# Fused attention, gated feed-forward and DFT mixing: 64-bit weights become 32-bit in three VectorE steps instead of four, and the scheduler is handed smaller pieces of the exponentials and of the w_out products

## The chip, the cores and the metric

The kernel runs on one core of one Trainium2 chip. Its engines, with the names that the profile gives them, are TensorE (PE, with its weight loads as PEld), VectorE (DVE), ScalarE (ACT), GpSimd (POOL) and SyncE (SP), which issues the DMAs of this kernel. Each engine works through its own instructions in the order in which they were written; engines wait for one another through semaphores. The metric is the device time of one launch in microseconds (us), the median of three runs.

## The reference

Inputs are q, k, v of shape (8, 8, 576, 64) in 32-bit floats, and w_in, conv_w, w_out, w_ch1 and w_ch2 in 64-bit floats. What is computed:

```python
# 1: attention inside chunks of 64 tokens, 8 heads of 64
scores = q_c @ k_c.T / 8;  attn = softmax(scores);  x = attn @ v_c      # x: (8, 576, 512)
# 2: gated feed-forward, 512 -> 1024 -> 512
h = relu(x @ w_in)
conv = sum_k conv_w[k] * h shifted by k - 1 tokens                       # 3 taps along the sequence
x = (h * sigmoid(conv)) @ w_out
# 3: mixing and a second feed-forward, 512 -> 2048 -> 512
u = x + real(fft over tokens and features of x)
un = (u - mean) / sqrt(var + 1e-6)
y = u + relu(un @ w_ch1) @ w_ch2
```

## The kernel before

The 4608 tokens (8 sequences of 576) are cut into ten blocks: block 0 of 256 tokens, blocks 1 to 8 of 512, block 9 of 256. For each block:

- `attention` (two pairs of heads at a time, q = 0 and 1): PE makes the scores (L393), DVE takes their maxima (L398, L399), ACT takes exponentials in instructions of 64 columns with their sums (L404), DVE divides (L407 to L409), PE turns the result (L418), ACT copies it out of PSUM (L421); then `values` multiplies by v on PE (L435) and ACT and DVE split the result into a high and a low part (L442, L444).
- `m_step`, eight times (f = 0 to 7): x @ w_in[f] on PE (L459 in block 0, where the weights are used as plain 32-bit floats; L468 in later blocks, where weight and input are each split in two and three products are summed), relu on ACT (L493), the middle tap on ACT (L498), the outer taps on DVE (L488), tanh on ACT (L505), the gate on DVE (L507), the split of the result (L279 on ACT, L280 on DVE).
- `x_step`, eight times: gate @ w_out[f] on PE into four PSUM accumulators, one bank for each 128 output features (L531 in block 0, L537 later). One scheduled operation holds all four banks' matmuls.

Behind the blocks come the DFT (`fold`, `d_step`, `s_step`, `u_step`; L602 to L730) and the second feed-forward by a seven-product scheme (`group`, L933; `second`, L1000), for which `weight_sums` and `weight_sums_late` prepare w_ch1 and w_ch2.

Every weight tile is loaded as 128 x 512 64-bit words into a wide buffer (L270, on SP) and turned into 32-bit floats by `to_float32` (L287 to L296). There are 48 such tiles: 8 of w_in and 8 of w_out during block 0, 16 of w_ch1 during blocks 1 to 8, 16 of w_ch2 during `group`. With them goes one small tile of conv_w. On the upper 32-bit word of each number DVE shifts and masks (L292), DVE adds the two top bits (L293), ACT takes the absolute value (L294); DVE adds the lower word's bits (L295), and DVE multiplies by zero where the absolute value is too small (L296). The ACT step writes over the scratch tile that L293 reads, so it stands behind L293. Scratch tiles are `wx` (one buffer) and `wf` (two). The 32-bit results of block 0 live in borrowed buffers whose names the rows below show: t, t, u, u, f00, f10, f01, f11, fz, ds0, ds1, xlo, xhi, dd0, dd1, fw, for w_in 0, w_out 0, w_in 1, w_out 1, and so on to w_out 7; the wide buffers are dd, dd, fw, wide, wide in turn. After its use in block 0 each weight is split into a high and a low part (`split_weight`: L279 on ACT, L280 on DVE, tiles wih, wil, woh, wol).

No order is written out. `Plan` (L114 to L209) collects operations with an engine, a cost from a formula, a priority and the buffers read and written, and `emit` plays them through a list scheduler with these costs: on each engine, of the operations that could start, the one of lowest priority number goes next. The order in which it emits them is the order of the engines' queues. So a change of one operation's cost, size or inputs can move operations everywhere. Accumulators o and x of PSUM have four buffers each.

Of the kernel before, what the change touches and what calls it, by code (L numbers as in the profile page):

```python
# [8 lines left out]
F32 = mybir.dt.float32  # L9
# [12 lines left out]
DT = 4  # L22
# [22 lines left out]

ORDER = (B11, B21, T2, T1, T3, B22, T4)

LEAST_NORMAL = 1.125 * 2.0**-15


class Buf:
# [175 lines left out]
def kernel(  # L227
# [44 lines left out]
    def vop(n, fn, prio, r, w, fast=False, scalars=0):  # L272
        return op("DVE", dve_cost(n, fast, scalars), fn, prio, r=r, w=w)

    def aop(n, fn, prio, r, w, psum=False, scalars=0, after=()):
        return op("ACT", act_cost(n, psum, scalars), fn, prio, r=r, w=w, after=after)
# [10 lines left out]
    def to_float32(f, x, wide, n, prio, view=lambda t: t):  # L287

        word = lambda t, k: t.rearrange("p (n two) -> p n two", two=2)[:, :, k]
        lo, hi = lambda: word(wide().bitcast(U32), 0), lambda: word(wide().bitcast(U32), 1)  # L290
        ff, fb, xb = lambda: view(f()), lambda: view(f()).bitcast(U32), lambda: x().bitcast(U32)
        vop(n, lambda: dve.tensor_scalar(xb(), hi(), 3, 0x3FFFFFF8, op0=ALU.logical_shift_left, op1=ALU.bitwise_and), prio, [wide], [x], fast=True)  # L292
        vop(n, lambda: dve.scalar_tensor_tensor(fb(), in0=hi(), scalar=0xC0000000, in1=xb(), op0=ALU.bitwise_and, op1=ALU.bitwise_or), prio, [wide, x], [f])  # L293
        aop(n, lambda: act.activation(out=x(), in_=word(wide().bitcast(F32), 1), func=ACT.Abs), prio, [wide], [x])  # L294
        vop(n, lambda: dve.scalar_tensor_tensor(fb(), in0=lo(), scalar=29, in1=fb(), op0=ALU.logical_shift_right, op1=ALU.bitwise_or), prio, [wide, f], [f])  # L295
        vop(n, lambda: dve.scalar_tensor_tensor(ff(), in0=x(), scalar=LEAST_NORMAL, in1=ff(), op0=ALU.is_ge, op1=ALU.mult), prio, [x, f], [f])  # L296


    def weight(pool_name, tag, bufs):
# [71 lines left out]
    def attention(i, q, prio, last):  # L371
        nw = SIZE[i] // 256
        n = 4 * nw
        blk = AT[i] // 256
        half = (slice(0, 64), slice(64, 128))
        qks, v = [], []
        for p in range(2):
            qks.append(buf(*(("s", "xlo", 2) if i + q == 1 and not i else ("a", "qk", 2)), [128, nw, 2, 256]))
            load(qks[p], lambda p=p: qk[blk:blk + nw, 2 * q + p].rearrange("w r a t -> r w a t"), 262144 * nw, prio - 12 + p)
        for p in range(2):  # L380
            v.append(buf("a", "v", 4, [128, nw, 256]))
            load(v[p], lambda p=p: v_in[blk:blk + nw, 2 * q + p].rearrange("w r t -> r w t"), 131072 * nw, prio - 10 + p)

        s = [buf("ps", "o" if i else "x", 4, [128, n, 64]) for _ in range(2)]

        def qk_unit():
            for w in range(nw):
                for j in range(2):
                    for p in range(2):
                        for u in range(2):  # L390
                            for h in range(2):
                                t, ks = qks[p](), slice(64 * (2 * j + u), 64 * (2 * j + u) + 64)
                                pe.matmul(s[h]()[half[u], 4 * w + 2 * p + j, :], t[half[h], w, 0, ks], t[half[h], w, 1, ks], start=True, stop=True)  # L393

        op("PE", 310 + 470 * nw, qk_unit, prio, r=qks, w=s)
        es, mx, sm = buf("a", "es", 1, [128, 2 * n, 64]), buf("a", "mx", 1, [128, 2, n]), buf("a", "sm", 1, [128, 2 * n, 1])
        for h in range(2):
            vop(64 * n, lambda h=h: dve.tensor_reduce(out=mx()[:, h, :], in_=s[h](), op=ALU.max, axis=AX.X), prio, [s[h]], [mx])  # L398
        vop(2 * n, lambda: dve.tensor_scalar(mx(), mx(), -0.125, None, op0=ALU.mult), prio, [mx], [mx])  # L399

        for h in range(2):
            def exp(h=h):
                for k in range(n):
                    act.activation(out=es()[:, n * h + k, :], in_=s[h]()[:, k, :], func=ACT.Exp, scale=0.125, bias=mx()[:, h, k:k + 1], accum_out=sm()[:, n * h + k, :])  # L404

            op("ACT", 291 * n, exp, prio, r=[s[h], mx], w=[es, sm])
        vop(2 * n, lambda: dve.tensor_scalar(sm(), sm(), 1e-9, None, op0=ALU.add), prio, [sm], [sm])  # L407
        vop(2 * n, lambda: dve.reciprocal(out=sm(), in_=sm()), prio, [sm], [sm])
        vop(128 * n, lambda: dve.tensor_tensor(es(), es(), sm().to_broadcast([128, 2 * n, 64]), op=ALU.mult), prio, [es, sm], [es])  # L409

        at = buf("a", "at", 2, [128, n, 128])
        for c in range(nw):
            tps = buf("ps", "o", 4, [128, 4, 128])

            def tr_unit(c=c, tps=tps):
                flat = es().rearrange("p a k -> p (a k)")
                for k in range(4):
                    pe.transpose(tps()[:, k, :], flat[:, 512 * c + 128 * k:512 * c + 128 * k + 128], ident)  # L418

            op("PE", 436, tr_unit, prio + 2, r=[es], w=[tps], spare=1)  # L420
            aop(512, lambda c=c, tps=tps: act.copy(out=at()[:, 4 * c:4 * c + 4, :], in_=tps()), prio + 2, [tps], [at], True)  # L421

        return lambda: values(i, q, nw, v, at, last)
# [94 lines left out]
    def x_step(i, f, prio):  # L518
# [7 lines left out]

        def x_unit(ds=range(DT)):
            if not i:
                for d in range(DT):
                    w = wf()[:, 128 * d:128 * d + 128]  # L530
                    pe.matmul(accs[d](), w, gh(), start=f == 0, stop=f == FT - 1)  # L531
                return
            wh, wl = wo[f][0](), wo[f][1]()
            for d in ds:
                dsl = slice(128 * d, 128 * d + 128)
                for k, (w, x) in enumerate(((wh, gh()), (wh, gl()), (wl, gh()))):
                    pe.matmul(accs[d](), w[:, dsl], x, start=f == 0 and k == 0, stop=f == FT - 1 and k == 2)  # L537

        end = i == NBLK - 1
        if not end or f < FT - 4:  # L540
            done = op("PE", mm_cost(no, passes=12 if i else 16), x_unit, prio, r=[*wo[f], gh, gl] if i else [wf, gh], w=accs)
        else:

            for k in range(2):
                x_last[k] = op("PE", mm_cost(no, passes=6), lambda k=k: x_unit((k, k + 2)), prio + k, r=[*wo[f], gh, gl], w=accs[k::2])
# [493 lines left out]
    for i in range(NBLK):  # L1039
        t, u, step = place(i, 0), place(i + 1, 0) if i + 1 < NBLK else 0, SIZE[i] / 288  # L1040
        if i + 1 < NBLK:
            rest = [attention(i + 1, q, *((t + (u - t) * (0.05 + 0.4 * q), u - 1.5 + 0.3 * q) if i else (t - 3.5 + 3 * q, t + 0.5 + 3 * q))) for q in range(2)]
            if not i:
                heads(1)
                for finish in rest:
                    finish()
# [186 lines left out]
```

## Time and profile before

| what | value |
|---|---|
| three runs | 1333.87, 1335.10, 1335.55 us; median 1335.1 |
| the profiled execution | 1334.92 us, of which 1333.1 from its first to its last instruction (the span) |
| busy, share of the span | PE 97%, PEld 87%, DVE 77%, ACT 57%, POOL 8% |
| granted TensorE clock, mean | 0.995 of full speed |

The profile lists for each engine how long its instructions ran. Matmuls overlap, so a PE that is shown as busy throughout is one that never waited. For a chain of cause and effect one reads the idle time before an instruction and what released it, which the profile puts in square brackets. On DVE and ACT consecutive instructions overlap a little: the distance from start to start is shorter than the duration.

### The profile page before, as it was taken

Reading aid. Unit: us, or ns where it says so; the run is one execution under the profiler, and the core shown is the slowest. Engines: PE = TensorE matmul, PEld = TensorE weight load, DVE = VectorE, ACT = ScalarE, POOL = GpSimd, SP = SyncE. Lnnn points to the kernel's source line nnn. Section 1 sums busy time; section 2 is a strip of 40 time slices with the busy share of each in tenths; the row PEclk is TensorE's granted clock in tenths of the full one; section 3 lists DMA queues with packets and bytes.
Section 4 is the critical chain, followed back from the end, with each engine's and each line's share of the span. In section 5 each row is a group of like instructions: output and inputs, shape, how many; then the busy total and the mean of one; then the engine's idle time right before and its main releaser. Section 6 shows DMA issues by size and latency. Waiting matters only on the chain.

```text
span 1333.1 us, 26136 instructions
## 1 busy us (share of the span) xinstructions
PE 1295.3 (97%) x9888; PEld 1165.2 (87%) x9888; DVE 1025.3 (77%) x1832; ACT 765.4 (57%) x1902; POOL 106.5 (8%) x247
## 2 busy tenths in 40 slices
PE   5899999999999999989999999999999999999998
PEld 3678888788888888979999888888899999999998
DVE  7997979878886786886978767674598877777873
ACT  5968767657775765665756557566643333333331
POOL 0121312201120220210000000000000000000000
PEclk9999999999999999998999999999999999999999
DMA  9435142434413031347775856778655355455441
GB/s 322 155 128 175 45 147 92 159 107 143 163 57 100 17 111 60 90 146 224 222 213 180 232 182 197 217 221 281 186 181 178 124 175 166 136 174 151 151 143 41
DMA packets 155327, 206.29 MB, mean 155 GB/s; under 512 B 10304, under 2 KB 103104, under 8 KB 155200
## 3 DMA queue, kind: packets, MB, share of 16 engines
q1 hardware_dynamic: 155200, 204.61, 48.7%
q8 instruction: 78, 1.28, 0.4%
q14 instruction: 49, 0.40, 0.1%
HBM read 130.51 MB, written 74.06 MB: 153 GB/s over the span
## 4 chain that ended last, share of the span: by engine, by line
PE 87%; DVE 7%; ACT 4%; issue 1%; DMA 0%; SPq 0%; POOL 0%; ACTq 0%; DVEq 0%
PE x L933 22%; PE x L1000 16%; PE o L468 13%; PE x L537 12%; PE o L1000 12%; PE o L933 4%; PE o L666 2%; PE o L699 2%; DVE cv L488 1%; PE o L721 1%; PE o L832 1%; PE o L393 1%; PE o L418 1%; PE o L435 1%; ACT es L404 1%
## 5 line engine op out<-in xcount | busy, mean ns | idle before, releaser
L279 ACT CAST sxh<-raw 128x1024 fp32r<-128x1024 f32 (+1 forms) x143 | 146.1, 1028 | 193.5 <-PE o L1000 84.3
L280 DVE TENSOR_TENSOR sxl<-raw,sxh 128x1024 fp32r<-128x1024 f32 (+1 forms) x143 | 169.4, 1194 | 27.0 <-ACT sxh L279 27.0
L933 PE MATMUL x<-sxh,th 128*128 128x512 f32 (+1 forms) x480 | 177.4, 370 | 0.9 <-ACT sum L917 0.6
L933 PE MATMUL x<-sxh,tl 128*128 128x512 f32 (+1 forms) x480 | 176.4, 368 | 0.0
L933 PE MATMUL x<-sxl,th 128*128 128x512 f32 (+1 forms) x480 | 176.3, 367 | 0.0
L468 PE MATMUL o<-x,wih 128*128 128x512 f32 (+1 forms) x576 | 172.4, 383 | 1.9 <-ACT at L421 0.7
L1000 PE MATMUL x<-tl,sxh 128*128 128x256 f32 x576 | 163.0, 283 | 0.0
L1000 PE MATMUL x<-th,sxl 128*128 128x256 f32 x576 | 163.0, 283 | 0.0
L1000 PE MATMUL x<-th,sxh 128*128 128x256 f32 x576 | 163.0, 283 | 0.0
L488 DVE SCALAR_TENSOR_TENSOR cv<-h,cw,cv 128x1 f32<-128x1 f32 (+30 forms) x272 | 129.1, 494 | 23.6 <-ACT cv L498 22.9
L468 PEld LDWEIGHTS o<-x,wih 128*128 128x128 f32 x576 | 103.9, 188 | 21.8 <-ACT h L493 1.6
L1000 PE MATMUL o<-th,sxh 128*128 128x256 f32 x432 | 122.3, 283 | 0.0
L1000 PE MATMUL o<-tl,sxh 128*128 128x256 f32 x432 | 122.3, 283 | 0.0
L1000 PE MATMUL o<-th,sxl 128*128 128x256 f32 x432 | 122.3, 283 | 0.0
L537 PE MATMUL x<-gh,woh 128*128 128x512 f32 (+1 forms) x288 | 111.5, 387 | 0.0
L1000 PEld LDWEIGHTS x<-th,sxh 128*128 128x128 f32 x576 | 110.6, 192 | 0.2
L1000 PEld LDWEIGHTS x<-tl,sxh 128*128 128x128 f32 x576 | 110.6, 192 | 0.0
L1000 PEld LDWEIGHTS x<-th,sxl 128*128 128x128 f32 x576 | 110.6, 192 | 0.0
L537 PE MATMUL x<-gl,woh 128*128 128x512 f32 (+1 forms) x288 | 109.5, 380 | 0.6 <-DVE gl L280 0.6
L537 PE MATMUL x<-gh,wol 128*128 128x512 f32 (+1 forms) x288 | 109.2, 379 | 0.0
L468 PE MATMUL o<-x,wil 128*128 128x512 f32 (+1 forms) x288 | 109.1, 379 | 0.0
L909 DVE TENSOR_TENSOR u<-x,u 128x256 f32<-128x256 f32 (+2 forms) x112 | 55.8, 499 | 66.8 <-PE x L1000 38.3
(280 smaller groups left out, 2957.2 us busy)
## 6 DMA issues: line engine op xcount, KB each, us to landing
raw<-h_scr SPq DMA_DIRECT2D x72, 512.0 KB, 5.2
h_scr<-sum SPq DMA_DIRECT2D x72, 256.0 KB, 3.1
u<-u_scr SPq DMA_DIRECT2D x66, 256.0 KB, 3.4
qk<-in_qk SPq DMA_DIRECT2D x32, 512.0 KB, 5.0
h_scr<-sum SPq DMA_DIRECT2D x48, 192.0 KB, 2.5
out_y<-u SPq DMA_DIRECT2D x35, 256.0 KB, 2.6
v<-in_v_in SPq DMA_DIRECT2D x32, 256.0 KB, 3.6
wide<-in_w_ch SPq DMA_DIRECT2D x16, 512.0 KB, 4.3
```

The costliest lines, as they stand in the source:

```text
L279: aop(n, lambda: act.copy(out=cut(h()), in_=cut(src())), prio, [src], [h], psum, after=after)
L280: vop(n, lambda: dve.tensor_tensor(cut(l()), cut(src()), cut(h()).bitcast(F32), op=ALU.subtract), prio, [src, h], [l])
L393: pe.matmul(s[h]()[half[u], 4 * w + 2 * p + j, :], t[half[h], w, 0, ks], t[half[h], w, 1, ks], start=True, stop=True)
L404: act.activation(out=es()[:, n * h + k, :], in_=s[h]()[:, k, :], func=ACT.Exp, scale=0.125, bias=mx()[:, h, k:k + 1], accum_out=sm()[:, n ...
L468: pe.matmul(acc(), w[:, ws], x, start=k == 0, stop=k == 11)
L488: vop(hi - lo, lambda: dve.scalar_tensor_tensor(cv()[:, lo:hi], in0=h()[:, off + k - 1 + lo:off + k - 1 + hi], scalar=tap(k), in1=cv()[:, ...
L537: pe.matmul(accs[d](), w[:, dsl], x, start=f == 0 and k == 0, stop=f == FT - 1 and k == 2)
L666: pe.matmul(acc()[:rows, :], x, w, start=k == 0 and n == 0, stop=k == 1 and n == 2)
L699: pe.matmul(accs[sine]()[:rows, :], w, x, start=n == 0, stop=n == len(todo) - 1)
L909: vop(n, lambda: dve.tensor_tensor(cut(x()), acc(), cut(x()), op=ALU.add), prio, [acc, x], [x])
L933: pe.matmul(acc(), a, b, start=first and m == 0, stop=m == 5, skip_group_check=not first)
L1000: pe.matmul(acc(), a, b, start=first and m == 0 and gs[0] == 0, stop=gs[-1] == FG - 1 and m == len(todo) - 1, skip_group_check=not first)
```

## The change

There are three edits.

1. `to_float32` begins on ACT: the upper word, read as a 32-bit float, is multiplied by 2**-112 into the scratch tile. Then DVE shifts and masks that tile into the result (a `tensor_scalar`), adds the lower word's bits and adds the sign bit (two `scalar_tensor_tensor`). There are three DVE instructions and one ACT instruction for a tile, where there were four and one.
2. The exponentials of an attention step are handed to the scheduler four at a time; before, they were handed over as all 4 or 8 of a half.
3. Each bank of an `x_step` is an operation of its own, with its own accumulator; before, one operation held four banks. The last four steps of block 9 stay as they were.

The last hunk of the diff adds a term that is zero.

```diff
-LEAST_NORMAL = 1.125 * 2.0**-15
+REBIAS = 2.0**-112
...
-        lo, hi = lambda: word(wide().bitcast(U32), 0), lambda: word(wide().bitcast(U32), 1)
-        ff, fb, xb = lambda: view(f()), lambda: view(f()).bitcast(U32), lambda: x().bitcast(U32)
-        vop(n, lambda: dve.tensor_scalar(xb(), hi(), 3, 0x3FFFFFF8, op0=ALU.logical_shift_left, op1=ALU.bitwise_and), prio, [wide], [x], fast=True)
-        vop(n, lambda: dve.scalar_tensor_tensor(fb(), in0=hi(), scalar=0xC0000000, in1=xb(), op0=ALU.bitwise_and, op1=ALU.bitwise_or), prio, [wide, x], [f])
-        aop(n, lambda: act.activation(out=x(), in_=word(wide().bitcast(F32), 1), func=ACT.Abs), prio, [wide], [x])
+        lo = lambda: word(wide().bitcast(U32), 0)
+        fb, xb = lambda: view(f()).bitcast(U32), lambda: x().bitcast(U32)
+        aop(n, lambda: act.mul(x(), word(wide().bitcast(F32), 1), REBIAS), prio, [wide], [x])
+        vop(n, lambda: dve.tensor_scalar(fb(), xb(), 3, 0x7FFFFFF8, op0=ALU.logical_shift_left, op1=ALU.bitwise_and), prio, [x], [f], fast=True)
         vop(n, lambda: dve.scalar_tensor_tensor(fb(), in0=lo(), scalar=29, in1=fb(), op0=ALU.logical_shift_right, op1=ALU.bitwise_or), prio, [wide, f], [f])
-        vop(n, lambda: dve.scalar_tensor_tensor(ff(), in0=x(), scalar=LEAST_NORMAL, in1=ff(), op0=ALU.is_ge, op1=ALU.mult), prio, [x, f], [f])
+        vop(n, lambda: dve.scalar_tensor_tensor(fb(), in0=xb(), scalar=0x80000000, in1=fb(), op0=ALU.bitwise_and, op1=ALU.bitwise_or), prio, [x, f], [f])
...
-            def exp(h=h):
-                for k in range(n):
+            def exp(ks, h=h):
+                for k in ks:
...
-            op("ACT", 291 * n, exp, prio, r=[s[h], mx], w=[es, sm])
+            for ks in (range(k, k + 4) for k in range(0, n, 4)):
+                op("ACT", 291 * 4, lambda exp=exp, ks=ks: exp(ks), prio, r=[s[h], mx], w=[es, sm])
...
-            done = op("PE", mm_cost(no, passes=12 if i else 16), x_unit, prio, r=[*wo[f], gh, gl] if i else [wf, gh], w=accs)
+            if i:
+                for d in range(DT):
+                    done = op("PE", mm_cost(no, passes=3), lambda d=d: x_unit([d]), prio, r=[*wo[f], gh, gl], w=[accs[d]])
+            else:
+                for d in range(DT):
+                    done = op("PE", mm_cost(no, passes=4), lambda d=d: x_unit([d]), prio, r=[wf, gh], w=[accs[d]])
```

In the listings below a changed kernel's line is up to five higher or two lower than that of before: its L292 is the ACT step, L293 to L295 are the DVE steps, L392 is the scores, L397 the maxima and L403 the exponentials; from L405 to L532 the numbers agree.

VectorE in block 0, before: conversions of w_in 4 (fz) and w_out 4 (ds_499), outer taps (cv), and behind them the sums of the first exponentials of block 1 (sm):

```order
L293 SCALAR_TENSOR_TENSOR fz<-wide,wf 128x512
L295 SCALAR_TENSOR_TENSOR f_471<-fw,f_471 128x512
L295 SCALAR_TENSOR_TENSOR fz<-wide,fz 128x512
L488 SCALAR_TENSOR_TENSOR cv<-h,cw,cv 128x253
L292 TENSOR_SCALAR wx<-wide 128x512
L488 SCALAR_TENSOR_TENSOR cv<-h,cw,cv 128x254
L293 SCALAR_TENSOR_TENSOR ds_499<-wide,wx 128x512
L280 TENSOR_TENSOR wil<-t,wih 128x512
L407 TENSOR_SCALAR sm<-sm 128x16
```

VectorE ahead of the same sums now (f_457 is w_in 3, gh the first gate):

```order
L280 TENSOR_TENSOR wil<-t,wih 128x512
L488 SCALAR_TENSOR_TENSOR cv<-h,cw,cv 128x253
L488 SCALAR_TENSOR_TENSOR cv<-h,cw,cv 128x254
L293 TENSOR_SCALAR f_457<-wx 128x512
L294 SCALAR_TENSOR_TENSOR f_457<-dd_330,f_457 128x512
L295 SCALAR_TENSOR_TENSOR f_457<-wx,f_457 128x512
L507 SCALAR_TENSOR_TENSOR gh<-cv,h 128x254
L407 TENSOR_SCALAR sm<-sm 128x16
```

A tile has one DVE instruction less, and its first one now reads the scratch tile that ACT wrote. Before, ten of the sixteen conversions had begun ahead of sm (L407); now sm and the first gate stand behind seven.

ScalarE at the same place, before (h is the first relu of block 0, es the first exponentials of block 1):

```order
L294 ACTIVATE wf<-wide 128x512
L294 ACTIVATE wx<-wide 128x512
L442 COPY gl<-o 128x2x128 x2
L294 ACTIVATE wf<-dd_254 128x512
L294 ACTIVATE wx<-dd_324 128x512
L493 ACTIVATE h<-o 128x256
L279 CAST wih<-t 128x512
L404 ACTIVATE es,sm<-o,mx 128x64 x8
```

ScalarE there now:

```order
L292 ACTIVATE wf<-wide 128x512
L442 COPY gl<-o 128x2x128 x2
L292 ACTIVATE wf<-dd_261 128x512
L493 ACTIVATE h<-o 128x256
L279 CAST wih<-t 128x512
L498 ACTIVATE cv<-h,cw 128x254
L403 ACTIVATE es,sm<-o,mx 128x64 x4
L292 ACTIVATE wx<-dd_330 128x512
L403 ACTIVATE es,sm<-o,mx 128x64 x4
```

The relu h no longer stands behind two weight steps that wait for DVE, and a weight's ACT step stands between groups of four exponentials.

TensorE at the end of block 0, before (L531 with fw is w_out 7, the last step of block 0; L468 is block 1):

```order
L459 MATMUL o<-gl,dd_820 128x256 x4
L531 MATMUL x<-gh,dd_810 128x254 x4
L435 MATMUL o<-at,v 64x64 x32
L393 MATMUL o<-qk 64x64 x32
L531 MATMUL x<-gh,fw 128x254 x4
L468 MATMUL o<-x_720,wih 128x512
```

TensorE there now (dd_774 is w_out 6; the steps of block 1 have twelve matmuls each, of which three stand here):

```order
L531 MATMUL x<-gh,xlo 128x254 x4
L392 MATMUL o<-qk 64x64 x32
L459 MATMUL o<-gl,dd_833 128x256 x4
L468 MATMUL o<-x_629,wih 128x512
L468 MATMUL o<-x_639,wih 128x512
L468 MATMUL o<-x_629,wil 128x512
...
L531 MATMUL x<-gh,dd_774 128x254 x4
```

Two steps of block 1 (24 matmuls of 512 columns) now stand ahead of block 0's last step, and the second L393 of block 2 stands behind it.

## Rows read from the trace of the kernel before

**Rows 1.** The page: busy time, share of the span and instructions of each engine.

```profile
PE 1295.3 (97%) x9888; PEld 1165.2 (87%) x9888; DVE 1025.3 (77%) x1832; ACT 765.4 (57%) x1902; POOL 106.5 (8%) x247
```

**Rows 2.** By stretch: length, busy PE, PEld, DVE, ACT, POOL; clock, DMA share, GB/s.

```profile
0.00:72.33 72.33, 49.01 (x664) 39.09 (x665) 63.12 (x137) 53.46 (x203) 8.61 (x16) 0.98 0.68 231
9.57:68.47 58.90, 42.32 (x538) 33.56 (x542) 58.33 (x126) 46.35 (x173) 5.59 (x9) 1.00 0.68 235
70.00:72.00 2.00, 2.00 (x12) 1.64 (x7) 2.00 (x5) 1.88 (x6) 0.93 (x1) 0.66 0.39 101
100.00:600.00 500.00, 490.54 (x4259) 418.49 (x4257) 399.90 (x832) 335.79 (x1109) 92.03 (x221) 1.00 0.33 108
235.00:255.00 20.00, 17.91 (x268) 14.88 (x268) 16.00 (x32) 10.52 (x44) 3.13 (x7) 1.00 0.69 216
560.00:600.00 40.00, 35.02 (x261) 33.21 (x259) 33.23 (x72) 25.60 (x66) 8.14 (x28) 0.96 0.37 127
640.00:972.00 332.00, 331.73 (x1654) 290.64 (x1654) 234.39 (x436) 208.27 (x388) 0.00 (x0) 1.00 0.69 208
```

**Rows 3.** TensorE in order of time: start, length, instruction, idle before and its releaser.

```profile
12.55 1.09 PE L418 MATMUL o<-ident,es 128*128 128x128 f32 x4 [4.94 <-DVE es L409]
19.45 1.06 PE L418 MATMUL o<-ident,es 128*128 128x128 f32 x4
28.76 1.99 PE L459 MATMUL o<-gl,f 128*128 128x256 f32 x8 [1.68 <-ACT h L493]
39.25 1.16 PE L393 MATMUL o<-qk 64*64 64x64 f32 x62 [0.55 <-ACT at L421]
62.44 1.88 PE L531 MATMUL x<-gh,dd 128*128 128x254 f32 x8
68.20 1.98 PE L393 MATMUL o<-qk 64*64 64x64 f32 x62 [1.29 <-DVE x L444]
70.11 2.57 PE L531 MATMUL x<-gh,fw 128*128 128x254 f32 x8
72.33 0.82 PE L468 MATMUL o<-x,wih 128*128 128x512 f32 x2
243.06 1.16 PE L435 MATMUL o<-at,v 64*64 64x64 f32 x62 [1.32 <-DVE x L444]
```

**Rows 4.** VectorE in order of time.

```profile
9.57 0.43 DVE L292 TENSOR_SCALAR wx<-dd 128x512 uint32<-128x512 uint32 x1 [3.47 <-DMA dd<-in_w_in]
30.18 0.67 DVE L293 SCALAR_TENSOR_TENSOR f<-fw,wf 128x512 uint32<-128x512 uint32 x1
30.79 0.67 DVE L293 SCALAR_TENSOR_TENSOR fz<-wide,wf 128x512 uint32<-128x512 uint32 x1
34.92 0.15 DVE L407 TENSOR_SCALAR sm<-sm 128x16 f32<-128x16 f32 x1
68.06 0.41 DVE L507 SCALAR_TENSOR_TENSOR gh<-cv,h 128x254 f32<-128x254 f32 x1
```

**Rows 5.** Groups by line and form: count, busy us, mean ns, idle before.

```profile
L293 DVE SCALAR_TENSOR_TENSOR wf<-wide,wx 128x512 uint32<-128x512 uint32 x16 | 11.0, 685 | 0.1
L292 DVE TENSOR_SCALAR wx<-wide 128x512 uint32<-128x512 uint32 x19 | 8.0, 419 | 0.0
L827 DVE TENSOR_SCALAR u<-u,mv,r 128x512 f32<-128x512 f32 x30 | 15.3, 543 | 0.4
L294 ACT ACTIVATE wx<-wide 128x512 f32<-128x512 f32 x19 | 13.4, 707 | 2.9 <-DVE wf L293 2.9
```

**Rows 6.** ScalarE in order of time.

```profile
16.39 0.25 ACT L404 ACTIVATION_READ_ACCUMULATOR es<-x,mx 128x1 f32 x1
27.78 0.66 ACT L294 ACTIVATE wx<-dd 128x512 f32<-128x512 f32 x1 [2.37 <-DVE f L293]
28.34 0.37 ACT L493 ACTIVATE h<-o 128x256 f32<-128x256 f32 x1
```

**Rows 7.** The chain that ended last: start, length, engine, tile, line, count.

```profile
72.68 5.48 PE o L468 x24
```

**Rows 8.** DMA issue of w_out 7, in 57 to 63: count, KB, us to landing.

```profile
wide<-in_w_out SPq DMA_DIRECT2D x1, 512.0 KB, 3.6
```

More of the change, by code (lines that the diff above doesn't have):

```diff
@@ L528, in x_unit @@
             if not i:
-                for d in range(DT):
+                for d in ds:
                     w = wf()[:, 128 * d:128 * d + 128]
@@ L1041 @@
         if i + 1 < NBLK:
-            rest = [attention(i + 1, q, *((t + (u - t) * (0.05 + 0.4 * q), u - 1.5 + 0.3 * q) if i else (t - 3.5 + 3 * q, t + 0.5 + 3 * q))) for q in range(2)]
+            rest = [attention(i + 1, q, *((t + (u - t) * (0.05 + 0.4 * q + 0 * (i == 1)), u - 1.5 + 0.3 * q) if i else (t - 3.5 + 3 * q, t + 0.5 + 3 * q))) for q in range(2)]
             if not i:
```

## Prediction

> **What bounds the kernel now.** I began with the page's busy shares: PE is busy for 97% of the span, DVE for 77% [rows 1]. So DVE work that goes is worth something only where PE waits for DVE. The busy times by stretch say where that is [rows 2]: up to 72.33 us PE is busy for 49.01 and idle for 23.3; in 100 to 600 it is idle for 9.5, of which 5.0 lie in 560 to 600; in 640 to 972 for 0.3. In 9.57 to 68.47, from the first weight's first DVE step to the last gate of block 0, DVE is busy for 58.33 of 58.90. There DVE sets the pace. The order of time on DVE [rows 4] shows the two ends, and start-to-start spacings: a step of 512 columns takes 0.67 us but 0.61 from the next (30.18, 30.79). PE's order of time [rows 3] shows the other side: waits for es, h and x of 4.94, 1.68 and 1.29 us, and its last L531 (w_out 7) runs right behind the last gate.
>
> **The parts and their costs.**
>
> *One DVE step less.* 48 instructions of 685 ns go [rows 5], 32.9 us of DVE. For the 32 tiles of w_ch1 and w_ch2 I count nothing: they lie where PE is busy for 490.5 of 500 and 331.7 of 332 us [rows 2]; PE's matmuls are the cover, and nothing here takes that away. The 16 tiles of block 0 count: 16 x 0.603 = 9.6 us. In the changed order, four other 512-column steps have come ahead of the last gate (two L280, one L444, one closing conversion step), 2.4 us. DVE's work ahead of the last gate falls by 7.2, from 57.3 to 50.1 (my sum of spacings).
>
> *The steps that remain.* L292 reads the scratch tile instead of every second word. The trace lacks this form; its nearest rows are the old one at 419 ns and L827, the same size with two more operands, at 543 [rows 5]. I take 419, the same operation; the end is +0.12 x 16 = 2 us of DVE, and as far below. The sign step has the operation pair and size of the step removed, 685 ns. The ACT step: L294 at 707 ns has the same form [rows 5]; I take no difference, and ±0.1 x 16 = 1.6 us of ACT as ends.
>
> *ACT now goes first.* A tile's DVE work cannot begin before ACT has reached its step, and ACT works in order. Before, the dependence ran the other way and cost too: L294 waited 2.37 us for DVE, h behind it, and PE 1.68 for h [rows 6, 3]. I walk the changed order, each instruction at the spacings above, held until its inputs exist.
> - The first exponentials end at the same time in either kernel. DVE now divides at once, so the first L418 comes 0.9 earlier, at 11.65 instead of 12.55 [rows 3]. The second pair's exponentials end at 15.8 instead of 16.64 [rows 6].
> - Three ACT steps stand behind these in ACT's order, so DVE has nothing from 13.4 to 15.8: 2.4 us lost. But es no longer stands behind conversions, and the second L418 starts near 16.9 instead of 19.45 [rows 3].
> - From there DVE's clock is its work so far plus 12.05. At the sums of block 1's first exponentials (L407) DVE arrives at 29.7 and ACT, which has a weight step among the 16 exponentials, is done at 31.7: another 2.0 lost, though before this came at 34.92 [rows 4]. Small waits for L505 and L442 bring the offset to 15.3; before, it ended at 10.8.
> - The last gate then ends at 50.1 + 15.3 + 0.3 = 65.7 against 68.47. So DVE alone brings 2.8, the rest of its saving being lost to waits for ACT.
> - PE gains more, because two steps of block 1 stand ahead of the end of block 0 and fill what it waits. By the walk it is busy without a wait from 58.5 on, does the last w_in step, 12 L468, 4 L531, 12 L468 and reaches w_out 7 at 67.4, ending at 69.2. In the kernel before the same work is done at 72.33, where L468 first starts [rows 3], plus the 5.48 that 24 of them take [rows 7], 77.8, less the 1.16 of the one L393 group that now comes later: 76.6. Gain 7.4.
> - The walk is too quick: with the same spacings, before's DVE comes to 66.3 at its last gate (57.3 of work, 9.0 of waits) and the trace has 68.06. For the part behind 31.7 that is about 1.0. I take a gain of 6.4.
>
> *The clock.* In 70 to 72 the granted clock is 0.66 [rows 2], so part of the time at the lower of its two levels, 1.2 GHz, after PE had waited 1.29 us [rows 3]; an L393 group took 1.98 us that takes 1.16 at the full clock, and the last L531 2.57 instead of 1.88. These 1.5 us lie inside the 7.4, as my walk runs at full clock. The Trainium skill, "TensorE: Matmul & The Clock Gate", Part 1, has the clock throttled by default and released by activity; by that rule the loss goes if these waits go, and stays if others come; the trace agrees that it fell behind waits. With the loss left the gain would be 4.9.
>
> *DMA.* SP's order is nearly the same. The one that comes close is w_out 7: it waits for DVE's lower-word step of w_out 6, by the walk at 54.4, and needs 3.6 to land as before [rows 8], to 58.0; ACT wants it at 57.6 to 58.1. I count nothing; a landing 2 us later stops ACT and the last gate by up to that.
>
> *Pieces of four and single banks.* The same instructions in finer order. Each x_step has the same matmuls, so PE's own work does not change. What can change is the 9.5 us of waits in 100 to 600. From the last DFT's L666 on, the order on PE is nearly that of before, so 5.0 stay. The other 4.5 may go, or grow: at 235 to 255, a block's end, PE is idle for 2.1, of which 1.32 is attention's L435 behind x [rows 2, 3]. I take no change; the ends are -4.5 and +2.1 for a further block like that.
>
> *Sum.* 1334.92 of the profiled execution (0.2 below the median of the runs) less 6.4: 1328.5. With the walk's ideal offset kept at 12.05, PE would end block 0 at 66.0, a gain of 10.6: 1324.3. With DVE's 2.8 alone: 1332.1.
>
> **The rivals.**
>
> *ACT takes DVE's place.* Then ACT's order decides: weight steps wait behind groups of exponentials and for landings, all else behind them. For it: ACT is busy for 46.35 of 58.90 in the same stretch [rows 2], its work up to the last gate does not fall, and in my walk DVE already loses 4.4 us to it. Against: 12.5 us of slack, part of which was its own wait for DVE. PE then has only DVE's 2.8: 1332.1. The Trainium skill ("TensorE: Matmul & The Clock Gate", the paragraph on engine queue depths) calls ScalarE's queue strictly first in, first out. The trace agrees: h, whose input stood ready, started only behind L294's 2.37 us [rows 6].
>
> *Block 0 is a chain, not DVE's load.* PE's waits before 72 are also for ACT and for landings, as 4.94 behind the first es; if the chain of scores, exponentials, turn and values sets the pace, DVE's relief does nothing, and only the early 0.9 stays: 1334.0. Against: DVE's 58.33 of 58.90, and the walk, in which that chain comes sooner.
>
> *Later blocks lose.* The finer pieces let the list scheduler put L418, L435 and L393 among single banks of L537, close behind what they need by its formulas. If every one of the eight later block ends had the 2.1 us of idle PE that 235 to 255 has, seven more would cost 14.7: 1334.9 - 6.4 + 14.7 = 1343.2, slower. It decides from 6.4 / 7 = 0.9 us a block on. For it: that stretch exists. Against: the other blocks' ends together have under 2.5, and their order, though finer, keeps some 11 us of PE work between scores and their turn.
>
> *Both gain.* If the later 2 to 4.5 us go as well: 1324 to 1326.5.
>
> **How the numbers follow.** The forecast, 1328.5 with its own range of 1325.5 to 1331.5, gets 0.60; ACT in DVE's place 0.16; the chain 0.08; later losses 0.08; both gain 0.08. Two parts in a thousand, 2.7 us, are about what a measurement of this kernel tells from no change, so faster means below 1332.4. Forecast and both-gain lie there wholly, 0.68, and of the ACT rival, whose centre is 1332.1, three quarters: 0.80 in all. The rest of it and the chain are the same: 0.12; slower 0.08. The range goes from 1323.5 (the ideal walk and a little of the later waits) to 1334.5 (the chain with some noise), leaving out the slower case and the tails.
>
> **What would show it.** In the changed profile, up to 75 us: no L293 of the old form; first L418 near 11.7 and a second near 17; DVE idle near 13 to 16 before a conversion's first step, released by ACT; L407 of block 1 near 32 behind exponentials; last gate at 64 to 68; last L531 at 68 to 71 with 24 L468 ahead of it; PE idle up to there 16 to 19 us, not 23.3; granted clock near 1.0 around 65 to 72. DVE's total falls to about 992, ACT's stays near 765, PE's near 1295. The forecast is wrong if w_out 7 still ends behind 73 us, if PE's idle in 100 to 600 differs from 9.5 by more than 4, or if DVE's steps of 419 and 685 ns change.

## The result, and the profile after

The changed kernel takes 1318.34 us (median of four runs, 1316.69 to 1320.66), the kernel before 1334.62 in the same session (1333.87 to 1335.55). The ratio is 0.9883, with a 95% interval of 0.9865 to 0.9900. A gain was forecast, but of 6.4 us; the measured one is 16.3, and 1318.34 lies below the predicted range of 1323.5 to 1334.5. The profiled execution was the slowest of the four, 1320.66, so its trace holds 14.3 us of the gain.

The page after, busy times as in [rows 1]: DVE has lost 27 us, and PE is still the engine that is never long idle.

```profile
PE 1290.2 (98%) x9888; PEld 1163.1 (88%) x9888; DVE 998.0 (76%) x1783; ACT 764.5 (58%) x1902; POOL 111.8 (8%) x247
```

The stretches that answer to [rows 2], in the same columns. Up to the end of block 0 PE is idle for 18.2 us instead of 23.3. In 70 to 72 the clock is 1.00 instead of 0.66. In 100 to 600 PE is idle for 5.50 us instead of 9.46, and all but 0.04 of that lies in 560 to 600: 235 to 255 has none.

```profile
0.00:69.94 69.94, 51.72 (x624) 41.30 (x625) 55.86 (x123) 53.61 (x203) 10.20 (x18) 1.00 0.73 249
70.00:72.00 2.00, 2.00 (x11) 1.62 (x10) 2.00 (x6) 2.00 (x8) 0.00 (x0) 1.00 0.00 0
100.00:600.00 500.00, 494.50 (x4296) 425.12 (x4295) 396.09 (x826) 331.66 (x1082) 93.99 (x219) 0.99 0.34 110
235.00:255.00 20.00, 20.00 (x213) 16.40 (x212) 14.64 (x28) 15.94 (x69) 2.44 (x5) 1.00 0.45 150
560.00:600.00 40.00, 34.54 (x212) 32.11 (x211) 31.48 (x63) 20.36 (x52) 4.52 (x16) 0.87 0.38 119
```

TensorE of the changed kernel in order of time, against [rows 3]: the first two turns of es (L418) came 0.88 and 2.40 us sooner, and the last L531 ended at 69.94, where the first L468 behind it starts.

```profile
11.67 1.09 PE L418 MATMUL o<-ident,es 128*128 128x128 f32 x4 [3.61 <-DVE es L409]
17.05 1.11 PE L418 MATMUL o<-ident,es 128*128 128x128 f32 x4 [1.30 <-DVE es L409]
30.01 1.97 PE L459 MATMUL o<-gl,f 128*128 128x256 f32 x8 [2.25 <-DVE f L295]
63.98 1.87 PE L531 MATMUL x<-gh,dd 128*128 128x254 f32 x8
68.41 1.88 PE L531 MATMUL x<-gh,fw 128*128 128x254 f32 x8
69.94 0.82 PE L468 MATMUL o<-x,wih 128*128 128x512 f32 x2
```

Its VectorE, against [rows 4]: the idle time in front of the two L407 is ended by ACT's exponentials, and the last gate starts at 66.15 instead of 68.06.

```profile
15.79 0.17 DVE L407 TENSOR_SCALAR sm<-sm 128x8 f32<-128x8 f32 x1 [2.60 <-ACT es L403]
32.11 0.17 DVE L407 TENSOR_SCALAR sm<-sm 128x16 f32<-128x16 f32 x1 [1.91 <-ACT es L403]
66.15 0.42 DVE L507 SCALAR_TENSOR_TENSOR gh<-cv,h 128x254 f32<-128x254 f32 x1
```

Its groups, against [rows 5]: the sign step and the step of ACT cost what the nearest rows said.

```profile
L295 DVE SCALAR_TENSOR_TENSOR wf<-wx,wf 128x512 uint32<-128x512 uint32 x16 | 11.0, 686 | 0.1
L293 DVE TENSOR_SCALAR wf<-wx 128x512 uint32<-128x512 uint32 x16 | 6.8, 426 | 0.4 <-ACT t L713 0.4
L292 ACT ACTIVATE wx<-wide 128x512 f32<-128x512 f32 x19 | 13.3, 702 | 1.2 <-DVE wf L295 0.6 <-DMA wide<-in_w_out 0.6
```

**Where the time went.** Kernels with other orders have other work ahead of the end of block 0, so that end is compared with equal work: 5.48 us off for 24 L468 that came ahead [rows 7], 1.16 on for an L393 group that comes later. For the changed kernel this is 69.94 - 5.48 + 1.16 = 65.62 against 72.33: 6.7 us. The second part is read at the first matmul of the second feed-forward (L933): 592.29 us before and 577.77 after, 14.5 sooner, so 7.8 us came between block 0 and there. The span is 14.2 shorter; behind that point nothing changed by more than 0.3. So the gain has two parts, and the second one is missing from the forecast.

**The second part in one block end.** This is TensorE in the stretch around the wait of 1.32 us at 243.06 [rows 3], before. All the waits between 240.48 and 252.28 (where the pair of 251.71 hands on) are 1.32 + 0.16 + 0.36 + 0.25 = 2.09 us.

```profile
240.48 1.26 PE L435 MATMUL o<-at,v 64*64 64x64 f32 x66
...
244.14 1.89 PE L699 MATMUL o<-ab,ds 128*64 128x258 f32 x14
246.00 0.32 PE L393 MATMUL o<-qk 64*64 64x64 f32 x2
246.48 1.15 PE L393 MATMUL o<-qk 64*64 64x64 f32 x62 [0.16 <-ACT t L705]
247.99 0.73 PE L468 MATMUL o<-x,wih 128*128 128x512 f32 x2 [0.36 <-DVE x L444]
...
251.71 0.72 PE L468 MATMUL o<-x,wih 128*128 128x512 f32 x2 [0.25 <-ACT h L493]
```

The same work in the changed kernel, without a wait: all 128 matmuls of L435 together, 12 of L537, the 14 of L704, 12 L468 and the scores.

```profile
227.49 2.09 PE L435 MATMUL o<-at,v 64*64 64x64 f32 x128
229.51 0.50 PE L537 MATMUL x<-gh,woh 128*128 128x512 f32 x1
...
232.37 1.83 PE L704 MATMUL o<-ab,ds 128*64 128x258 f32 x14
234.03 0.64 PE L468 MATMUL o<-x,wih 128*128 128x512 f32 x2
234.51 0.40 PE L468 MATMUL o<-x,wil 128*128 128x512 f32 x1
...
236.88 1.16 PE L392 MATMUL o<-qk 64*64 64x64 f32 x64
237.97 0.63 PE L726 MATMUL o<-ident,xlo 128*64 128x128 f32 x4
238.35 0.48 PE L537 MATMUL x<-gh,woh 128*128 128x512 f32 x1
```

From start to start these took 2.02 for L435, 1.66 for L704, 2.85 for 12 L468, 1.09 for the scores, 0.38 for L726 and 0.48 for a pair of L468: 8.48 us for what took 252.28 - 240.48 = 11.80 before. The loss was 3.3 us where the trace showed 2.1 of waits. That fits the lengths in the trace: an L468 or L537 is shown as 0.39 us long, but the next one starts 0.23 behind it when nothing holds it, so the first 0.16 us of a wait would not be shown. So 4.5 us of shown waits can well be 7.8 us of time.

### The profile page after: what moved, and what is told of

It is laid out like the page before. It is cut to its first block, busy times and chain, and to the rows that moved or that the text cites. A ratio compares the mean times of both kernels' runs of the same rounds, so it can differ in the third digit from the quotient of the medians.

```text
span 1318.9 us, 26083 instructions
## 1 busy us (share of the span) xinstructions
PE 1290.2 (98%) x9888; PEld 1163.1 (88%) x9888; DVE 998.0 (76%) x1783; ACT 764.5 (58%) x1902; POOL 111.8 (8%) x247
## 4 chain that ended last, share of the span: by engine, by line
PE 93%; DVE 3%; ACT 2%; DMA 1%; issue 1%; SPq 0%; ACTq 0%; DVEq 0%
PE x L938 22%; PE x L1005 16%; PE x L537 14%; PE o L468 14%; PE o L1005 12%; PE o L938 4%; PE o L671 3%; PE o L704 2%; PE o L726 1%; PE o L837 1%; PE o L435 1%; PE o L392 1%; PE o L418 1%; ACT es L403 1%; DMA ts<-t_scr 0%
## 5 line engine op out<-in xcount | busy, mean ns | idle before, releaser
L468 PE MATMUL o<-x,wih 128*128 128x512 f32 (+1 forms) x576 | 172.2, 382 | 0.0
L488 DVE SCALAR_TENSOR_TENSOR cv<-h,cw,cv 128x512 f32<-128x512 f32 (+30 forms) x272 | 129.2, 495 | 32.4 <-ACT cv L498 32.1
L468 PEld LDWEIGHTS o<-x,wih 128*128 128x128 f32 x576 | 104.7, 188 | 19.5
L537 PE MATMUL x<-gh,woh 128*128 128x512 f32 (+1 forms) x288 | 112.4, 390 | 0.0
L537 PE MATMUL x<-gl,woh 128*128 128x512 f32 (+1 forms) x288 | 109.2, 379 | 0.0
L537 PE MATMUL x<-gh,wol 128*128 128x512 f32 (+1 forms) x288 | 109.2, 379 | 0.0
L468 PE MATMUL o<-x,wil 128*128 128x512 f32 (+1 forms) x288 | 108.9, 378 | 0.0
```

The source lines that it names most:

```text
L468: pe.matmul(acc(), w[:, ws], x, start=k == 0, stop=k == 11)
L488: vop(hi - lo, lambda: dve.scalar_tensor_tensor(cv()[:, lo:hi], in0=h()[:, off + k - 1 + lo:off + k - 1 + hi], scalar=tap(k), in1=cv()[:, ...
```

## The experiments

A is edit 1 (three steps), B edit 2 (exponentials by four), C edit 3 (w_out steps by bank). "Idle" is PE's idle time in 100 to 560 us; "block 0" is the end of block 0 with equal work; "second" is the start of the second feed-forward, all from the profiled execution. The medians come from several sessions, in which the kernel before took 1332.9 to 1334.6 us, so kernels are compared by the ratios. No kernel leaves out any work.

| kernel | median us | ratio to before (95%) | block 0 | idle | second |
|---|---|---|---|---|---|
| before | 1334.62 | 1 | 72.3 | 4.48 | 592.3 |
| A | 1334.21 | 1.0008 (0.9999 to 1.0017) | 69.6 | 6.93 | 591.3 |
| B | 1326.06 | 0.9945 (0.9933 to 0.9958) | 67.0 | 3.02 | 584.6 |
| C | 1328.32 | 0.9957 (0.9942 to 0.9972) | 71.0 | 2.77 | 586.8 |
| AB | 1326.54 | 0.9946 (0.9934 to 0.9958) | 67.1 | 4.02 | 587.5 |
| AC | 1321.01 | 0.9912 (0.9899 to 0.9925) | 68.9 | 0.24 | 579.9 |
| BC | 1320.91 | 0.9911 (0.9898 to 0.9925) | 67.9 | 0.28 | 580.4 |
| ABC, the changed kernel | 1318.34 | 0.9883 (0.9865 to 0.9900) | 65.6 | 0.04 | 577.8 |

**The edits one by one and by twos.** Each kernel is that of before with the hunks of the change named. `e1_three_steps` (A):

```diff
-        aop(n, lambda: act.activation(out=x(), in_=word(wide().bitcast(F32), 1), func=ACT.Abs), prio, [wide], [x])
+        aop(n, lambda: act.mul(x(), word(wide().bitcast(F32), 1), REBIAS), prio, [wide], [x])
...
```

> The kernel before with the first edit alone: three VectorE steps for each weight, exponentials and w_out steps handed over as before. Load theory (the shorter conversions free VectorE, in block 0 and in the blocks behind it, and the short waits of TensorE go with it): nearly the whole gain, 1318 to 1322 us, TensorE idle in 100 to 560 us under 1 us. Order theory (block 0 gains by the shorter conversions, the later gain comes from the smaller pieces): 1327 to 1329 us, TensorE idle in 100 to 560 us near 4.5 us. Chance theory (any reshuffle of the list moves the later waits by some us either way): 1322 to 1332 us, with later waits unlike both.

Measured: no gain, above the ranges of all three theories. Its end of block 0 is 2.7 us sooner, close to the 2.8 at which DVE's relief alone was priced, but PE waits 2.4 us more behind it, as the row of 100 to 560 shows (columns as above):

```profile
100.00:560.00 460.00, 453.07 (x3992) 383.71 (x3991) 356.79 (x741) 307.45 (x1034) 80.33 (x193) 1.00 0.32 103
```

And no L468 stands ahead of its last L531: the reordering on which most of the forecast's gain in block 0 rested comes with edit 2 or with edit 3. B alone has 36 of them there, C alone 24.

`e2_small_pieces` (BC) has the two other edits and the old four steps:

```diff
+            for ks in (range(k, k + 4) for k in range(0, n, 4)):
+                op("ACT", 291 * 4, lambda exp=exp, ks=ks: exp(ks), prio, r=[s[h], mx], w=[es, sm])
...
+                    done = op("PE", mm_cost(no, passes=3), lambda d=d: x_unit([d]), prio, r=[*wo[f], gh, gl], w=[accs[d]])
```

> The kernel before with the second and third edits alone: exponentials by four, w_out steps by bank, four VectorE steps for each weight as before. Load theory: 1333 to 1336 us, last L531 near 72 us and TensorE idle in 100 to 560 us of 4 to 5 us. Order theory: 1326 to 1328 us, with the later waits gone and the end of block 0 as before. Chance theory: anywhere from 1326 to 1338 us.

Measured: 0.9911, three quarters of the gain without a single DVE step less. That is better than any of the three theories had it, 1320.91 us against 1326 at the lowest.

`e5_exp_by_four` (B):

```diff
-            op("ACT", 291 * n, exp, prio, r=[s[h], mx], w=[es, sm])
+            for ks in (range(k, k + 4) for k in range(0, n, 4)):
+                op("ACT", 291 * 4, lambda exp=exp, ks=ks: exp(ks), prio, r=[s[h], mx], w=[es, sm])
```

> The kernel before with the second edit alone: exponentials handed over four at a time. Bank theory (the w_out steps by bank make the gain of the small pieces): 1331 to 1336 us, TensorE idle in 100 to 560 us of 4 us or more. Exponential theory (shorter holds on ScalarE make it): 1320 to 1324 us, under 1 us idle there. Chance theory (any reshuffle does it or undoes it): 1322 to 1338 us, not additive with the next runs.

`e6_banks` (C):

```diff
-            done = op("PE", mm_cost(no, passes=12 if i else 16), x_unit, prio, r=[*wo[f], gh, gl] if i else [wf, gh], w=accs)
...
+                for d in range(DT):
+                    done = op("PE", mm_cost(no, passes=3), lambda d=d: x_unit([d]), prio, r=[*wo[f], gh, gl], w=[accs[d]])
```

> The kernel before with the third edit alone: each bank of a w_out step an operation of its own. Bank theory: 1319 to 1324 us, no waits in 100 to 560 us, the steps of block 1 ahead of the end of block 0. Exponential theory: 1331 to 1336 us. Chance theory: 1322 to 1338 us.

`e7_steps_banks` (AC) and `e8_steps_exp` (AB) are the changed kernel with one hunk undone each:

```diff
-            for ks in (range(k, k + 4) for k in range(0, n, 4)):
+            op("ACT", 291 * n, exp, prio, r=[s[h], mx], w=[es, sm])
```

```diff
-                for d in range(DT):
-                    done = op("PE", mm_cost(no, passes=3), lambda d=d: x_unit([d]), prio, r=[*wo[f], gh, gl], w=[accs[d]])
+            done = op("PE", mm_cost(no, passes=12 if i else 16), x_unit, prio, r=[*wo[f], gh, gl] if i else [wf, gh], w=accs)
```

> First and third edit together, exponentials in halves as before. Bank theory: 1316 to 1320 us, as the changed kernel. Exponential theory: 1330 to 1335 us, as the first edit alone. Chance theory: unlike both.

> First and second edit together, w_out steps whole as before. Bank theory: 1330 to 1335 us. Exponential theory: 1316 to 1320 us. Chance theory: unlike both.

Measured (table): B and C alone fit only the chance theory. AC comes 1 us above the range of the bank theory. AB lies between the two other theories, so again only chance is left.

What follows: with 1334 us for the ratios, the mean effect of each edit over the four settings of the others is -2.1 us for A (+1.1, +0.1, -6.0, -3.7), -6.4 for B (-7.3, -8.3, -6.1, -3.9) and -7.9 for C (-5.7, -12.8, -4.5, -8.4). A is worth something only beside C. Alone, B moves the end of block 0 most, by 5.4.

How B does that shows in its trace. The sums of block 1's first exponentials come at 34.84 us, no sooner than before (34.92, [rows 4]); in A alone they come at 31.14. This is the row of B, where the line is L408:

```profile
34.84 0.16 DVE L408 TENSOR_SCALAR sm<-sm 128x16 f32<-128x16 f32 x1
```

The last gate starts at 70.67, later than before (68.06). What is new is the 36 matmuls of block 1 that PE does while it waits for that gate: in 65 to 75 us PE has no idle time, where before it had 2.47 and a lower clock. The first row is of before, the second of B.

```profile
65.00:75.00 10.00, 7.53 (x111) 6.41 (x104) 10.00 (x20) 8.21 (x41) 2.32 (x1) 0.83 0.56 183
```

```profile
65.00:75.00 10.00, 10.00 (x46) 8.36 (x45) 10.00 (x22) 8.99 (x40) 5.25 (x4) 1.00 0.22 60
```

**Is it DVE's load or the order?** `e3_double_sign_late` issues the sign step a second time, which changes no value, for the 32 tiles of w_ch1 and w_ch2; `e4_double_sign_all` for all 48. The scheduler does not know of it, so the order on every engine stays that of the changed kernel.

```diff
-        vop(n, lambda: dve.scalar_tensor_tensor(fb(), in0=xb(), scalar=0x80000000, in1=fb(), op0=ALU.bitwise_and, op1=ALU.bitwise_or), prio, [x, f], [f])
+        def sign():
+            for _ in range(2 if prio > 8 else 1):
+                dve.scalar_tensor_tensor(fb(), in0=xb(), scalar=0x80000000, in1=fb(), op0=ALU.bitwise_and, op1=ALU.bitwise_or)
+
+        vop(n, sign, prio, [x, f], [f])
```

> The changed kernel with the same order on every engine, but the last VectorE step of a conversion issued twice (the second time it changes nothing) for the 32 tiles of w_ch1 and w_ch2 only: VectorE has its old number of instructions there, about 0.6 us more for each tile. Load theory: the later waits come back, 1324 to 1328 us. Order theory: 1317 to 1320 us, as the changed kernel. Chance theory makes no statement, as the order stays.

> As the third, but doubled for all 48 tiles, block 0's too. VectorE's queue of block 0 gets 16 x 0.6 = 9.6 us longer at the same order. Load theory: 1330 to 1335 us. Order theory: later as the changed kernel, in block 0 a loss of 5 to 8 us, 1323 to 1327 us; the last L531 at 74 to 77 us, where the changed kernel has 68.4.

Measured: 1323.66 (0.9935, 0.9921 to 0.9948) and 1335.96 (1.0024, 1.0016 to 1.0033). The first lies 0.3 us below the range of the load theory, the second 1.0 above it; the order theory is off by 3.7 and by 9. The 32 steps for which the forecast counted nothing cost 3 to 7 us when they come back into a fixed order (6.9 by the ratios, 5.3 by the medians, 2.9 at the second feed-forward of the profiled executions), and those of block 0 another 12: its last L531 ends at 82.16 instead of 69.94, for 16 x 0.6 = 9.6 us of DVE work. The granted clock up to there was 0.92 in `e4` and 1.00 in the changed kernel, so a part of the 12 may be the clock. In `e3` PE waits again, one wait being 1.46 us for es. So DVE's load does decide in an order made without it. But BC, whose order was made with the full load, takes 1320.91: a scheduler that knows of the load hides most of it.

**Which w_out steps matter?** A block's first w_out step could hand the accumulators over sooner, bank by bank; or the later steps could serve as filler for holes on PE. `e9_banks_first_step` splits only f = 0, `e10_banks_other_steps` only the others:

```diff
-            if i:
+            if i and not (f == 0):
+                done = op("PE", mm_cost(no, passes=12), x_unit, prio, r=[*wo[f], gh, gl], w=accs)
+            elif i:
```

(and `f > 0` in the second).

> The changed kernel, but in blocks 1 to 9 only a block's first w_out step (f = 0) is handed over by bank; the other steps are whole again. Hand-over theory (a whole first step must wait until the evictions of the block before have freed all four x banks, so single banks help at block starts): as the changed kernel, 1317 to 1321 us, no waits of TensorE in 100 to 550 us. Filler theory (small pieces anywhere let the list put attention's links and block starts where their inputs are ready): 1322 to 1328 us, 3 us of waits or more there. Chance: waits of 0 to 4 us unlike either.

> The mirror of the run before: in blocks 1 to 9 the first w_out step is whole, steps f = 1 to 7 go by bank. Hand-over theory: 1322 to 1328 us with waits at block starts. Filler theory: 1317 to 1321 us, under 1 us of waits in 100 to 550 us.

Measured: 1322.67 (0.9925, 0.9913 to 0.9937) and 1319.90 (0.9902, 0.9888 to 0.9916). The stretch of 100 to 560 us, of the first and then of the second kernel:

```profile
100.00:560.00 460.00, 456.10 (x4031) 387.07 (x4030) 361.76 (x754) 308.63 (x1022) 84.71 (x203) 1.00 0.32 105
```

```profile
100.00:560.00 460.00, 459.56 (x4068) 390.95 (x4067) 364.27 (x762) 311.00 (x1029) 84.29 (x203) 1.00 0.34 107
```

With the first step alone split, 3.90 us of waits are back, for instance this one, nearly as long as the worst of before:

```profile
196.45 0.73 PE L468 MATMUL o<-x,wih 128*128 128x512 f32 x2 [1.15 <-ACT h L493]
```

Block 0 ends at 65.9 and 66.0, as in the changed kernel. So the later steps, as filler, bring most of the gain. `e9` is still 2.8 us better than AB (0.9925 against 0.9946), 1.2 of it at the end of block 0; the rest is no more than a reshuffle moves, so a small part for the hand-over is neither shown nor ruled out.

**How much is luck of one order?** A scheduler's order moves with any number. `e11_reshuffled_before` raises the planner's price of an exponential in the kernel before from 291 to 295, `e13_reshuffled_after` in the changed one:

```diff
-            op("ACT", 291 * n, exp, prio, r=[s[h], mx], w=[es, sm])
+            op("ACT", 295 * n, exp, prio, r=[s[h], mx], w=[es, sm])
```

> The kernel before with one number of the planner changed (an exponential is put down as 295 instead of 291), the same work in a slightly other order: it measures how far a reshuffle alone moves the time. Order theory (the gains belong to the sizes of the pieces): within 2 us of before, waits in 100 to 550 us of 4 us or more. Chance theory: 4 us or more away on either side.

> The changed kernel, all of it, with the planner's price of four exponentials raised from 1164 to 1180, which changes nothing but the order. Bank theory (single banks of w_out behind the first step fill what PE would wait in 100 to 560 us, in nearly any order): the later waits stay away, PE idle under 0.5 us in 100 to 560, and the time is 1316 to 1322, ratio 0.987 to 0.991, with only block 0 moving by up to 3 us. Chance theory (the vanished waits are the luck of one order): idle comes back to 2 to 5 us and the time to 1322 to 1327.

Measured: 1332.21 (0.9993, 0.9984 to 1.0001) and 1317.40 (0.9882, 0.9867 to 0.9897). In `e11` the end of block 0 moved by 2.1 us one way and the later part by 2.9 the other, so a difference of 2 to 3 us between two orders in one part says nothing of a cause. Its waits in 100 to 560 are 2.22 us, not the 4 or more that the order theory had for it. In `e13` the waits stay away, and the end of block 0 is 64.9:

```profile
100.00:560.00 460.00, 459.82 (x4090) 393.72 (x4089) 364.63 (x763) 310.64 (x1032) 88.16 (x202) 1.00 0.33 108
```

**Is it the size of the piece, and must it be w_out?** `e14_two_banks` splits the w_out steps behind block 0 in two, `e15_w_in_halves_only` is AB with the w_in steps in two halves, and `e12_w_in_halves` puts the same halves on top of the changed kernel, to see if finer still is better.

```diff
-                for d in range(DT):
-                    done = op("PE", mm_cost(no, passes=3), lambda d=d: x_unit([d]), prio, r=[*wo[f], gh, gl], w=[accs[d]])
+                for d in (0, 2):
+                    done = op("PE", mm_cost(no, passes=6), lambda d=d: x_unit([d, d + 1]), prio, r=[*wo[f], gh, gl], w=accs[d:d + 2])
```

```diff
-            done = op("PE", mm_cost(n, passes=12), m_unit, prio, r=[*wi[f], *(t.buf for hp in range(0, HP, 2) for t in x0[i, hp])], w=[acc], after=m_last)
+            for hps in ((0, 1), (2, 3)):
+                done = op("PE", mm_cost(n, passes=6), lambda hps=hps: m_unit(hps), prio, r=[*wi[f], *(t.buf for t in x0[i, hps[0]])], w=[acc], after=() if hps[0] else m_last)
```

> The changed kernel with the w_out steps behind the first in two pieces of two banks each, not four of one. Bank theory with size mattering: a piece twice as long fits half as many holes, PE idle 0.5 to 3 us in 100 to 560 and a time between that of the changed kernel and that of the first step alone by bank, 1320 to 1323. Any-small-filler theory: a piece of six matmuls is small enough, idle under 0.5 us and 1317 to 1320.

> Three steps and exponentials by four, the w_out steps whole as before, but the w_in steps in two halves of six matmuls. Bank theory (it must be w_out, whose inputs lie ready while a w_in step waits on an accumulator and on weights): later waits stay, idle 2.5 to 5 us in 100 to 560, and the time is that of the kernel with three steps and exponentials by four, 1325 to 1328. Any-small-filler theory: idle under 0.8 us and 1318 to 1322.

> The changed kernel with the w_in steps of blocks 1 to 9 handed over in two halves as well (head pairs 0 and 1, then 2 and 3, each with its own input). Filler theory: nothing left to gain in 100 to 550 us, where the changed kernel has no waits, so 1316 to 1320 us, with up to 2 us less in block 0. Chance theory: waits come back, up to 1324 us.

Measured: `e14` 1323.38 (0.9923, 0.9909 to 0.9936), `e15` 1328.52 (0.9967, 0.9954 to 0.9979), `e12` 1317.95 (0.9887, 0.9872 to 0.9902). The stretch of 100 to 560 us, of `e14` and then `e15`:

```profile
100.00:560.00 460.00, 457.69 (x4054) 390.00 (x4053) 363.76 (x760) 310.89 (x1027) 82.75 (x203) 1.00 0.33 106
```

```profile
100.00:560.00 460.00, 456.24 (x4022) 386.52 (x4021) 361.57 (x752) 308.52 (x1022) 84.76 (x197) 1.00 0.32 104
```

Two banks leave 2.31 us of waits, half of before's; halves of w_in leave 3.76, no better than AB's 4.02, and their time is longer than AB's. Both times lie 0.4 to 0.5 us above the range that their bank theory gave. By the waits it must be w_out, but by time this is not shown: the second feed-forward of `e15` starts at 583.22 us, 4.3 sooner than AB's and 1.8 behind that of `e14` (581.42), and what makes `e15` slower than AB lies behind that point, where no w_in step is left (743.3 us to the end of the span against 738.6). `e12` is the same as the changed kernel: with 0.03 us of waits left there is nothing for finer pieces to fill, and none of these versions beats the changed kernel.

The fill can also be counted. In the order of time on PE between 72 and 580 us, all kernels have 864 matmuls of L537. Before, 2 runs of them are shorter than 12; after, 53 are (25 of 3, 12 of 6, 16 of 9); with two banks 41, all of 6. C alone has 55 and still 2.77 us of waits, so short runs alone do not end them.

## Why the prediction was right and wrong

**What held.** The walk of block 0: first L418 at 11.67 (11.65 forecast), second at 17.05 (16.9), sums of block 1 at 32.11 (31.7), last gate done at 66.6 (65.7), last L531 at 69.94 (69.2), with the 24 L468 ahead of it, gain with equal work 6.7 (6.4 taken, 7.4 by the ideal walk). PE's idle up to there is 18.2 (16 to 19). The clock term held: 1.00 in 70 to 72. DVE's total is 998 (about 992 forecast) and ACT's 764.5 (near 765); no conversion step's mean duration changed by more than 7 ns. With 6.7 us gained there, the rivals that left 2.8 (ACT in DVE's place) and 0.9 (the chain) fell.

**The step that failed** is "*Pieces of four and single banks* ... I take no change; the ends are -4.5 and +2.1". PE's waits in 100 to 560 went from 4.48 to 0.04 us, which is the whole lower end, and the time behind them is 7.8 us. Two things went wrong in it. First, I read finer pieces as the same work in finer order, with a gain or a loss equally likely. The runs show that they work as filler: of the kernels with the w_out steps behind a block's first in single banks, all but C alone have at most 0.44 us of waits there (AC, BC, ABC, `e10`, `e12`, `e13`), leaving out `e3` and `e4`, whose DVE load the order does not know; of those without, none has under 2.2. Second, the end of -4.5 took the waits as shown for the whole of the loss; the block end above lost 3.3 us for 2.1 shown. With 7.8 in its place the sum would be 1334.92 - 6.4 - 7.8 = 1320.7, and the profiled execution took 1320.66; that the two agree so closely is luck, as the term of block 0 is itself 0.3 off. Because the waits shown are only a part of the loss, the prediction's own sign of being wrong, waits in 100 to 600 that differ from 9.5 by more than 4, did not show: they fell by 3.96.

**A number that was right without its cause.** The forecast of 6.4 us in block 0 has two parts: 2.8 for DVE's relief, and the rest for two steps of block 1 that stand ahead of the end of block 0 and fill what PE waits. The first part held: A alone moves that end by 2.7, and 2.3 on top of B and C, though by nothing on top of B. But the second part comes with B and with C, each of which has such steps ahead without A, and A alone has none. The walk was made with the changed order as it stands, which holds all three edits, so it gave the right end without telling which edit made it, while edits 2 and 3 were put down as "no change". It was filler in block 0 as it was behind it.

**Rivals.** "Both gain" was the right one in kind, with 0.08; its price was the shown waits again. "Later blocks lose" is refuted: 235 to 255 has no idle time, and all of 100 to 560 has 0.04. Of the term for the 32 later tiles, "I count nothing", half is right: A's worth beside C, and `e3`, say that they can cost some us in an order that has no slack for them; BC says that a new order hides most of that.

**What stays open.** Why C alone keeps 2.77 us of waits while AC and BC have 0.24 and 0.28 is not settled. 2.1 of them are two waits of the DFT's L671 for a split by DVE (ab), the longest 1.81, so A can relieve them; but `e11` shows orders that differ by as much by chance, and C was run in one order only. The difference between BC and ABC is 2.6 us by the medians and 3.7 by the ratios. In the profiled executions it lies at the end of block 0 (67.9 against 65.6), about as far as `e11` moved that end, so that DVE makes it is likely and not shown. Why the scheduler puts steps of block 1 ahead of the end of block 0 in B, where block 1's first exponentials come no sooner, is open.

## What to carry to other kernels

Where a list scheduler sets the order and the bottleneck engine waits often and briefly, cut work whose inputs lie ready into the smallest pieces that cost nothing extra, and look for such work first. Here 12 matmuls of w_out became 4 times 3; together with the two other edits this took away 4.4 us of shown waits, 7.8 us of time. Price a vanished wait by the distance from start to start over the same work, not by the idle time shown. When several edits change one order, walk or run the order of each edit alone before naming the edit that pays.

## What the runs showed of the hardware

In these traces a wait on PE cost more than was shown. In the kernel before, this matmul was shown as waiting 0.19 us, yet it started 0.59 behind its forerunner, where the next two follow at 0.34 and 0.23:

```profile
395.63 0.40 PE L537 MATMUL x<-gh,woh 128*128 128x512 f32 x1
396.22 0.50 PE L537 MATMUL x<-gl,woh 128*128 128x512 f32 x1 [0.19 <-DVE gl L280]
396.56 0.39 PE L537 MATMUL x<-gh,wol 128*128 128x512 f32 x1
396.79 0.39 PE L537 MATMUL x<-gh,woh 128*128 128x512 f32 x1
```

The granted clock at the hand-over to the second feed-forward did not change, though the row of 560 to 600 seems to say so (0.87 against 0.96): aligned on the start of the second feed-forward (L933 of before), 23 us of before and of after read 0.85 both. The first row is of before, the second of after.

```profile
592.00:615.00 23.00, 19.95 (x109) 18.32 (x108) 17.14 (x31) 10.53 (x23) 0.00 (x0) 0.85 0.57 174
```

```profile
577.00:600.00 23.00, 19.90 (x111) 18.31 (x109) 17.63 (x32) 10.88 (x23) 0.00 (x0) 0.85 0.56 173
```

A row of fixed times in two kernels of unlike speed compares different work.
